# Attention chunks transposed by the DMA crossbar in place of TensorE, in a fused decay-attention and GELU-MLP kernel

## The chip, the cores and the metric

The kernel runs on one core of one Trainium2 chip. The metric is device time in microseconds for one launch; lower is better. Engines are written PE (TensorE), DVE (VectorE), ACT (ScalarE), POOL (GpSimd) and SP (SyncE, which here only issues DMAs).

## The reference

Linear attention with a per-head decay `lam`, in blocks, with a running state, then an MLP with exact GELU. Shapes: q, k, v are (4, 8, 768, 64); the MLP has 3072 tokens, 512 to 2048 to 512.

```python
for b in range(nb):
    qb, kb, vb = (q[:, :, sl], k[:, :, sl], v[:, :, sl])
    intra = np.einsum('bhic,bhjc->bhij', qb, kb) * Dmask[None]
    intra = np.einsum('bhij,bhjd->bhid', intra, vb)
    inter = np.einsum('bhid,bhde->bhie', qb * lam_pow[None], kv_state)
    out[:, :, sl] = intra + inter
    kb_dec = kb * rev_pow[None]
    kv_state = lam_block * kv_state + np.einsum('bhsd,bhse->bhde', kb_dec, vb)
x = out.transpose(0, 2, 1, 3).reshape(B * S, H * D)
h = x @ w_in
g = 0.5 * h * (1.0 + erf(h / sqrt(2)))
return g @ w_out
```

`Dmask[i, j]` is `lam ** (i - j)` for i >= j and 0 above; `lam_pow` is `lam ** (i + 1)`.

## The kernel before, in words

The sequence is cut into chunks of 128 positions of all 8 heads: 24 chunks, six per batch entry, so a chunk's place in its sequence `sb` runs from 0 to 5. Four chunks make a group (512 tokens), and there are six groups. The MLP works on one group at a time. While the MLP of group g runs, the attention of the four chunks of group g+1 is woven into it, so that TensorE always has matmuls to do. The four chunks of group 0 are done ahead (`early`).

A chunk has four steps:
- `begin`, kind 0: `prefetch(n + 4)` first issues the loads of q, k and v of the chunk four ahead on POOL's DMA queue (line 66; the load casts f32 to bf16). Then `decay_k` (L178) makes `k_dec` on POOL.
- `transposes`, kind 1: 8 TensorE transposes (L184), 4 of k and 4 of q (a pair of heads each), into a PSUM tile `t_ps`. DVE then copies the k half to `kT` (L190), and multiplies the q half by the row of decays `lam_q` into `qT` (L191).
- `scores`, kind 2: 8 matmuls `sc_ps` from `kT` and `qT` (L198), up to 8 matmuls `kv_ps` from `k_dec` and `v` (L205), the product with the mask on DVE (`sc_m`, L210), and the new state (L214 or L216). POOL then makes `old`, the decayed state, for the chunk after (L219); chunks with `sb` 4 and 5 have no `old`, and those with `sb` 5 no `k_dec`.
- `outputs`, kind 3: 8 matmuls from state and `qT` (L228), 8 from `v` and `sc_m` (L232), and a DVE cast into the MLP's input `x_t` (L238).

The MLP of a group is a list of 32 blocks of 4 matmuls: 16 blocks `mm1` (L250, each followed by a GELU on ACT, L252), then 16 blocks `mm2` (L262). Each four `mm2` blocks end one tile of 128 output rows, which ACT copies to SBUF (L267) and SP stores (L268, 256 KB).

The order of the instructions is the program's own, since the kernel runs under a manual schedule: each engine takes its instructions in the order in which they are written. A list `todo` gives each step of each chunk a position in the group's blocks. Chunk i's step with the fraction f stands at (i + f) of four equal intervals, which cover 97% of the group, so an interval is 7.76 blocks. Before each block, every step whose position has been reached is written out. For chunk i = 0 a negative fraction means the start of the group's list:

```python
at = lambda f: (first + (end - first) * (i + f) / M) * total
...
for run, cost in blocks:
    while todo and todo[0][0] <= done:
        _, kind, step = todo.pop(0)
        step(kind)
    run()
    done += cost
```

In groups g >= 1 of the loop, scores of chunk i stands at fraction 0.35: for the four chunks after 3, 11, 19 and 26 blocks. Outputs stand at 0.75. `kT`, `qT` and `k_dec` have three buffers each, the loaded q, k and v eight, and each engine waits only on semaphores, so POOL and SP may run ahead of TensorE.

Of the kernel before, what the change touches and what calls it, by code (L numbers as in the profile page):

```python
# [9 lines left out]
BF16 = mybir.dt.bfloat16  # L10
# [5 lines left out]
def kernel(  # L16
# [10 lines left out]
    nc = tc.nc  # L27

    B, H, S, D = q.shape
    d_model, d_ff = moe_w_in.shape  # L30
    C = 128
    NB = S // C
    NCH = B * NB
    HP = H // 2
# [15 lines left out]
    work_pool = ctx.enter_context(tc.tile_pool(name="work", bufs=3))  # L50
# [66 lines left out]
    lam_p = consts.tile([128, H], F32)  # L117
# [8 lines left out]
    for hi in range(2):  # L126
        p = slice(hi * D, (hi + 1) * D)
        nc.vector.tensor_copy(cpw[p], pw_r[p, :, :, hi])
    for b in range(LB):
        n = 2 ** b  # L130
# [24 lines left out]
    def bank(shape, dtype, tag, name):  # L155
        return ps.tile(shape, dtype, tag=tag, name=name, bufs=2 if tag in ("sc", "mh", "mo") else 1)

    def begin(n, early=False):
        c = Chunk()
        c.n, c.sb, c.early = n, n % NB, early  # L160
        c.sc_tag = "mo" if early and n % 2 else "sc"
        if n == 0:
            for name in "kq":
                raw[0, name] = qkv_pool.tile([128, H, D], BF16, tag=name, name=f"{name}_t")
                nc.scalar.copy(raw[0, name], first_f[name])  # L165
        c.q, c.k, c.v = (raw.pop((n, name)) for name in "qkv")
        return c

    def decay_k(c, eng):

        if c.sb == NB - 1:
            return
        c.k_dec = work_pool.tile([128, H, D], BF16, tag="kd", name="k_dec")
        if eng is nc.scalar:
            for h in range(H):
                nc.scalar.activation(c.k_dec[:, h, :], c.k[:, h, :], ACT.Copy, scale=lam_k[:, h:h + 1])
        else:
            eng.tensor_mul(c.k_dec, c.k, lam_k[:, :, None].to_broadcast((128, H, D)))  # L178

    def transposes(c):  # L180
        t_ps = bank([128, 2, HP, C], BF16, "mh" if c.early else "t", "t_ps")
        for i, src in ((0, c.k), (1, c.q)):
            for hp in range(HP):
                nc.tensor.transpose(t_ps[:, i, hp, :], src[:, 2 * hp:2 * hp + 2, :], ident)  # L184
        c.kT = work_pool.tile([128, HP, C], BF16, tag="kT", name="kT")
        c.qT = work_pool.tile([128, HP, C], BF16, tag="qT", name="qT")
        if c.early:
            nc.scalar.copy(c.kT, t_ps[:, 0])
        else:
            nc.vector.tensor_copy(c.kT, t_ps[:, 0])  # L190
        nc.vector.tensor_mul(c.qT, t_ps[:, 1], lam_q)  # L191

    def scores(c):
        sc_ps = [bank([128, HP, C], F32, c.sc_tag, f"sc_ps{hi}") for hi in range(2)]
        for hp in range(HP):
            for hi in range(2):
                p = slice(hi * D, (hi + 1) * D)
                nc.tensor.matmul(sc_ps[hi][:, hp, :], c.kT[p, hp, :], c.qT[p, hp, :], start=True, stop=True)  # L198
        more = c.sb < NB - 1
        if more:  # L200
            kv_ps = bank([128, HP, D], F32, "t", "kv_ps")
            for hp in range(HP):
                for hi in range(2):
                    h = 2 * hp + hi
                    nc.tensor.matmul(kv_ps[hi * D:(hi + 1) * D, hp, :], c.k_dec[:, h, :], c.v[:, h, :],  # L205
                                     start=True, stop=True)
        c.sc_m = work_pool.tile([128, HP, 2, C], BF16, tag="sc_m", name="sc_m")
        dmask_r = dmask.rearrange("p (hp hi) i -> p hp hi i", hi=2)
        for hi in range(2):
            nc.vector.tensor_mul(c.sc_m[:, :, hi, :], sc_ps[hi], dmask_r[:, :, hi, :])  # L210
        if more:
            new = work_pool.tile([128, HP, D], BF16, tag="state", name="state")
            if c.sb == 0:
                nc.vector.tensor_copy(new, kv_ps)  # L214
            else:
                nc.vector.tensor_add(new, kv_ps, states[c.n][1])  # L216
            old = work_pool.tile([128, HP, D], F32, tag="old", name="old")
            if c.sb < NB - 2:
                (nc.vector if c.early else nc.gpsimd).tensor_mul(old, new, lam_c_b)  # L219
            states[c.n + 1] = new, old  # L220

    def outputs(c, x_t, off):
        o_ps = bank([128, HP, C], F32, "o", "o_ps")
        if c.sb > 0:
            for hp in range(HP):
                for hi in range(2):
                    p = slice(hi * D, (hi + 1) * D)
                    nc.tensor.matmul(o_ps[p, hp, :], states[c.n][0][p, hp, :], c.qT[p, hp, :],  # L228
                                     start=(hp == 0), stop=False, skip_group_check=True)
        for hp in range(HP):  # L230
            for hi in range(2):
                nc.tensor.matmul(o_ps[hi * D:(hi + 1) * D, hp, :], c.v[:, 2 * hp + hi, :], c.sc_m[:, hp, hi, :],  # L232
                                 start=(c.sb == 0 and hp == 0), stop=True, skip_group_check=True)
        x_o = x_t[:, :, off * C:(off + 1) * C]
        if c.early:
            nc.scalar.copy(x_o, o_ps)  # L236
        else:
            nc.vector.tensor_copy(x_o, o_ps)  # L238
# [60 lines left out]
    def alloc_x(g):  # L299
        xT[g] = x_pool.tile([128, NK1, M * C], BF16, tag="x", name="x_t")  # L300
# [3 lines left out]
    def prefetch(upto):  # L304
        while next_load[0] <= min(upto, NCH - 1):
            for name in "kqv":
                load(next_load[0], name)
            next_load[0] += 1
# [3 lines left out]
    live = {}  # L312
    for s in range(M + 1):
        if s < M:
            live[s] = begin(s, early=True)
            if s == 2:
                load_w_in(0)
            transposes(live[s])
            decay_k(live[s], nc.scalar if s < 2 else nc.gpsimd)
            if s == 0:  # L320
                make_dmask()
        if s >= 1:
            outputs(live[s - 1], xT[0], s - 1)
        if s < M:
            scores(live[s])
# [5 lines left out]
    for g in range(NG):  # L331
        blocks = mlp_blocks(g)
        total = sum(c for _, c in blocks)
        todo = []
        if g + 1 < NG:
            alloc_x(g + 1)
            first, end = (0.77, 1.0) if g == 0 else (0.0, 0.97)
            for i in range(M):
                n = (g + 1) * M + i
                at = lambda f: (first + (end - first) * (i + f) / M) * total  # L340

                def step(kind, n=n, i=i):
                    if kind == 0:
                        prefetch(n + 4)
                        live[n] = begin(n)
                        decay_k(live[n], nc.gpsimd)
                    elif kind == 1:
                        transposes(live[n])
                    elif kind == 2:
                        scores(live[n])  # L350
                    else:
                        outputs(live[n], xT[g + 1], i)
                fs = (-0.3, 0.0, 0.4, 1.0) if g == 0 else (-0.3, 0.0, 0.35, 0.75)
                todo += [(at(f), kind, step) for kind, f in enumerate(fs)]
            todo.sort(key=lambda t: t[0])
        done = 0
# [6 lines that stand above are left out]
        for _, kind, step in todo:  # L363
            step(kind)
# [30 lines left out]
```

## Time and profile before

| | us |
|---|---|
| median of three runs | 242.4 (241.0 to 243.05) |
| profiled execution, whole | 242.4 |
| profiled execution, span of its instructions | 240.6 |
| PE busy in the span | 217.7 |
| POOL busy | 95.1 |
| DVE busy | 85.8 |
| ACT busy | 82.7 |

The span runs from the first to the last instruction of one profiled execution. Busy time is the time in which the engine has an instruction at work. In lines of groups or of the timeline, `kT<-t_ps` means that the tile left of the arrow is written from the one right of it; L190 is line 190 of the kernel; a bracket such as `[3.66 <-PE o_ps L262]` says how long the engine was idle before and what ended that. `SPq` is SP's queue of DMA issues. The MLP of group 1 starts at about 69 us, those of the later groups at 105, 140, 175 and 210 us; the tail of the program is the last group's MLP with no attention left in it.

### The profile page before, as it was taken

The numbers are of one execution on the slowest core, as the hardware profiler recorded it, in microseconds if no ns is written. First come the engines' busy times: TensorE is split into PE (matmuls) and PEld (weight loads), VectorE is DVE, ScalarE is ACT, GpSimd is POOL, SyncE is SP. The second block draws the span as 40 slices with busy tenths as digits, with TensorE's granted clock in tenths as the row PEclk, the third lists the DMA queues.
The fourth block names the chain that finished last, engine by engine and source line by source line (L and its number), as shares of the span: only waits on it lengthen the run. The fifth ranks groups of instructions, "written<-read, shape, count | busy, mean of one in ns | idle before, by whom it ended". The sixth has DMA issues, their size and how long they took to land.

```text
span 240.6 us, 4008 instructions
## 1 busy us (share of the span) xinstructions
PE 217.7 (90%) x1652; PEld 110.5 (46%) x1680; DVE 85.8 (36%) x180; ACT 82.7 (34%) x149; POOL 95.1 (40%) x114
## 2 busy tenths in 40 slices
PE   0378899998499999999999999999999999999994
PEld 0256344454254444455455455444454545444453
DVE  6987200057633423324344343343342344100000
ACT  3463266010025530135521035521055510166211
POOL 8986337970775296007347592007211200000000
PEclk9999999999869999999999999999999999999999
DMA  7999999995994799225598599009110002110022
GB/s 112 152 158 203 191 200 155 155 198 35 98 117 28 46 73 161 56 87 33 33 68 93 105 154 87 3 1 137 62 44 0 3 9 81 44 44 0 10 80 87
DMA packets 82865, 20.44 MB, mean 85 GB/s; under 512 B 75552, under 2 KB 79904, under 8 KB 82848
## 3 DMA queue, kind: packets, MB, share of 16 engines
q0 software_dynamic: 77024, 13.37, 74.4%
q1 hardware_dynamic: 4784, 6.56, 7.8%
q10 hardware_dynamic: 1040, 0.26, 0.5%
q8 instruction: 13, 0.21, 0.4%
q14 instruction: 4, 0.03, 0.0%
HBM read 27.27 MB, written 6.29 MB: 139 GB/s over the span
## 4 chain that ended last, share of the span: by engine, by line
PE 71%; POOL 12%; DMA 10%; issue 6%; ACT 0%; POOLq 0%
PE h_ps L250 29%; PE o_ps L262 28%; DMA w_out_t<-in_moe_w_out_dram 7%; POOL v_t L66 3%; PE t_ps L184 3%; DMA k_t<-in_k_dram 3%; POOL q_t L66 3%; PE o_ps L232 3%; PE o_ps L228 2%; PE sc_ps L198 2%; POOL k_t L66 2%; POOL k_dec L178 2%; PE kv_ps L205 2%; PE o_ps L277 1%; POOL w_in_t L93 1%
## 5 line engine op out<-in xcount | busy, mean ns | idle before, releaser
L250 PE MATMUL h_ps<-x_t,w_in_t 128*128 128x512 bf16 x371 | 88.8, 386 | 1.7 <-ACT x_t L236 0.7
L262 PE MATMUL o_ps<-w_out_t,g_t 128*128 128x512 bf16 x353 | 83.9, 383 | 1.4 <-issue 0.9
L252 ACT ACTIVATE g_t<-h_ps 128x512 bf16<-128x512 f32 x96 | 57.3, 597 | 45.1 <-PE h_ps L250 44.4
L250 PEld LDWEIGHTS <-w_in_t 128*128 128x128 bf16 x384 | 36.5, 99 | 43.3 <-issue 4.1
L262 PEld LDWEIGHTS <-g_t 128*128 128x128 bf16 x368 | 34.0, 98 | 37.9 <-issue 0.6
L267 ACT COPY o_sb<-o_ps 128x512 f32<-128x512 f32 x23 | 13.5, 585 | 92.8 <-PE o_ps L262 92.8
L210 DVE TENSOR_TENSOR sc_m<-sc_ps,dmask 128x512 bf16<-128x512 f32 x48 | 30.9, 686 | 31.4 <-PE sc_ps L198 31.3
L219 POOL TENSOR_TENSOR old<-state,cpw 128x256 f32<-128x256 bf16 x12 | 7.4, 613 | 81.4 <-DVE state L216 40.8
L238 DVE CAST x_t<-o_ps 128x512 bf16<-128x512 f32 x20 | 13.8, 692 | 38.7 <-PE o_ps L232 38.5
L190 DVE COPY kT<-t_ps 128x512 bf16<-128x512 bf16 x20 | 8.5, 423 | 48.6 <-PE t_ps L184 48.6
L66 POOL DMA_DIRECT2D v_t<-in_v_dram x24 | 21.5, 897 | 3.3 <-DMA w_out_t<-in_moe_w_out_dram 1.7
L66 POOL DMA_DIRECT2D q_t<-in_q_dram x23 | 20.5, 892 | 4.9 <-DMA w_out_t<-in_moe_w_out_dram 3.7
L66 POOL DMA_DIRECT2D k_t<-in_k_dram x23 | 20.9, 909 | 3.9 <-DMA w_out_t<-in_moe_w_out_dram 1.7
L178 POOL TENSOR_TENSOR k_dec<-k_t,lam_k 128x512 bf16<-128x512 bf16 x18 | 20.1, 1118 | 0.9 <-DMA k_t<-in_k_dram 0.7
L198 PE MATMUL sc_ps<-qT,kT 64*128 64x128 bf16 x192 | 10.4, 232 | 7.6 <-DVE qT L191 7.6
L191 DVE TENSOR_TENSOR qT<-t_ps,lam_q 128x512 bf16<-128x512 bf16 x24 | 16.3, 681 | 0.0
L184 PE MATMUL t_ps<-ident,k_t 128*128 128x128 bf16 x96 | 10.4, 238 | 5.9 <-DVE pw L124 5.9
L198 PEld LDWEIGHTS <-kT 64*128 64x128 bf16 x192 | 6.5, 99 | 16.1 <-issue 12.5
L184 PEld LDWEIGHTS <-k_t 128*128 128x128 bf16 x96 | 7.3, 104 | 10.3 <-ACT k_t L165 5.9
L232 PE MATMUL o_ps<-sc_m,v_t 128*64 128x128 bf16 x192 | 11.6, 243 | 0.2 <-DVE sc_m L210 0.2
L184 PE MATMUL t_ps<-ident,q_t 128*128 128x128 bf16 x96 | 10.5, 239 | 0.7 <-ACT q_t L165 0.7
L205 PE MATMUL kv_ps<-v_t,k_dec 128*64 128x64 bf16 x160 | 7.7, 213 | 2.2 <-POOL k_dec L178 2.2
(45 smaller groups left out, 80.3 us busy)
## 6 DMA issues: line engine op xcount, KB each, us to landing
out_dram<-o_sb SPq DMA_DIRECT2D x23, 256.0 KB, 2.0
v_t<-in_v_dram POOLq DMA_DIRECT2D x24, 128.0 KB, 4.9
k_t<-in_k_dram POOLq DMA_DIRECT2D x23, 128.0 KB, 4.7
q_t<-in_q_dram POOLq DMA_DIRECT2D x23, 128.0 KB, 5.0
w_in_t<-in_moe_w_in_dram POOLq DMA_DIRECT2D x4, 512.0 KB, 7.7
w_out_t<-in_moe_w_out_dram POOLq DMA_DIRECT2D x4, 512.0 KB, 15.1
k_first<-in_k_dram ACTq DMA_DIRECT2D x1, 256.0 KB, 4.5
q_first<-in_q_dram SPq DMA_DIRECT2D x1, 256.0 KB, 5.3
```

The source lines that it names most:

```text
L66: nc.gpsimd.dma_start(raw[n, name], chunk_of(name, n))
L178: eng.tensor_mul(c.k_dec, c.k, lam_k[:, :, None].to_broadcast((128, H, D)))
L184: nc.tensor.transpose(t_ps[:, i, hp, :], src[:, 2 * hp:2 * hp + 2, :], ident)
L191: nc.vector.tensor_mul(c.qT, t_ps[:, 1], lam_q)
L198: nc.tensor.matmul(sc_ps[hi][:, hp, :], c.kT[p, hp, :], c.qT[p, hp, :], start=True, stop=True)
L210: nc.vector.tensor_mul(c.sc_m[:, :, hi, :], sc_ps[hi], dmask_r[:, :, hi, :])
L232: nc.tensor.matmul(o_ps[hi * D:(hi + 1) * D, hp, :], c.v[:, 2 * hp + hi, :], c.sc_m[:, hp, hi, :], start=(c.sb == 0 and hp == 0), stop=Tru ...
L238: nc.vector.tensor_copy(x_o, o_ps)
L250: nc.tensor.matmul(h_ps, w_in_t[:, ki, kf * 128:(kf + 1) * 128], x_t[:, ki, :], start=(ki == 0), stop=(ki == NK1 - 1))
L252: nc.scalar.activation(g_t[:, kf, :], h_ps, ACT.Gelu)
L262: nc.tensor.matmul(om[io], g_t[:, kf, io * C:(io + 1) * C], w_out_t[:, kf, :], start=(kf == 0), stop=(kf == NK2 - 1))
L267: nc.scalar.copy(o_sb, om[io])
```

## The change

In the loop's passes g >= 1, which prepare groups 2 to 5 (chunks 8 to 23), the TensorE transposes and the two DVE operations after them are replaced by two DMA transposes on SP's queue. The decay of q, which was applied after the transposing, is applied before it, by POOL, with the column of decays `lam_p` in place of the row `lam_q`. The step that starts a chunk stands at the fraction -0.8 in these groups, not -0.3; the other positions stay. Groups 0 and 1 (chunks 0 to 7) are as before.

```diff
+    def dma_transposes(c):
+        c.kT = work_pool.tile([128, HP, C], BF16, tag="kT", name="kT")
+        c.qT = work_pool.tile([128, HP, C], BF16, tag="qT", name="qT")
+        q_hat = work_pool.tile([128, H, D], BF16, tag="qh", name="q_hat")
+        nc.sync.dma_start_transpose(out=c.kT, in_=c.k.rearrange("p h d -> p (h d)"))
+        nc.gpsimd.tensor_mul(q_hat, c.q, lam_p[:, :, None].to_broadcast((128, H, D)))
+        nc.sync.dma_start_transpose(out=c.qT, in_=q_hat.rearrange("p h d -> p (h d)"))
...
-                def step(kind, n=n, i=i):
+                def step(kind, n=n, i=i, g=g):
                     if kind == 0:
                         prefetch(n + 4)
                         live[n] = begin(n)
+                        if g > 0:
+                            dma_transposes(live[n])
                         decay_k(live[n], nc.gpsimd)
                     elif kind == 1:
-                        transposes(live[n])
+                        if g == 0:
+                            transposes(live[n])
...
-                fs = (-0.3, 0.0, 0.4, 1.0) if g == 0 else (-0.3, 0.0, 0.35, 0.75)
+                fs = (-0.3, 0.0, 0.4, 1.0) if g == 0 else (-0.8, 0.0, 0.35, 0.75)
```

The DMA transposes read SBUF and write SBUF: `kT` and `qT` have the same layout as before, 128 partitions (a pair of heads by 64) by 4 pairs by 128 positions.

## The prediction

> **What bounds the kernel now.** I read the page's busy times first, then the busy times by stage, then the chain of waits, and last the timeline around the four places where the chain could break. The first row of the page:
>
> ```profile
> PE 217.7 (90%) x1652; PEld 110.5 (46%) x1680; DVE 85.8 (36%) x180; ACT 82.7 (34%) x149; POOL 95.1 (40%) x114
> ```
>
> TensorE (PE) is busy for 90%, no other engine for half. The busy times by stage (cut at the first matmul of each MLP group) show how little is idle where the change acts:
>
> ```profile
> 105.30:140.20 34.90, 34.37 (x277) 17.06 (x280) 13.34 (x24) 11.84 (x21) 17.80 (x21) 1.00 0.73 72
> 140.20:174.90 34.70, 34.33 (x271) 16.89 (x274) 13.00 (x23) 11.87 (x21) 11.61 (x14) 1.00 0.70 70
> 174.90:209.60 34.70, 34.33 (x271) 16.79 (x274) 13.00 (x23) 11.67 (x20) 3.23 (x4) 1.00 0.09 31
> ```
>
> The columns are span, PE, weight load, DVE, ACT, POOL, clock, DMA share and GB/s. PE works 34.3 of 34.7 us at clock 1.00, so whatever is taken from its stream shortens the stage, and whatever it waits for lengthens it. The chain of waits confirms it; this is the boundary at 139.9 us:
>
> ```profile
> 138.20 1.67 PE o_ps L262 x7
> 139.88 0.45 PE t_ps L184 x8
> 140.32 2.59 PE h_ps L250 x12
> 142.91 0.33 PE sc_ps L198 x8
> 143.24 0.25 PE kv_ps L205 x8
> ```
>
> Each piece starts when the one before ends. Eight transposes of a chunk cost 0.445 us (0.056 each; the 238 ns of one in the table of groups is latency, not cost). After the boundary, three MLP blocks (12 matmuls, 2.59 us) are all that lies before the first chunk's scores.
>
> [...] a 256 KB store landed after 2.0 us beside nothing and after 3.4 us beside loads.
>
> **The change, part by part.**
>
> Removed from PE: 8 transposes for each of 16 chunks (8 to 23). Fifteen times 0.445 us is on the chain. At the first one (chunk 8, 68.8 us) the next matmul at 69.6 waited anyway for the x_t cast, which ends at 69.53, so it gives some 0.1. Sum: 15 x 0.445 + 0.1 = 6.8 us.
>
> Removed from DVE: 16 copies of 423 ns and 16 products of 681 ns, 17.7 us. DVE is busy 13 of 35 us per stage; this gives nothing to the chain.
>
> Added to POOL: 16 products q_hat of the same shape as k_dec, 1118 ns each, 17.9 us. POOL is busy at most 18 us of a stage. In its queue q_hat stands behind the chunk's three load issues (0.9 us each) and ahead of k_dec and of the next `old`. For chunks 1 to 3 of a group this is covered. The tightest is chunk 1 in the stage at 140 us: POOL ends the first chunk's step at about 140.7 (the 139.6 at which k_dec ends before, and 1.1), then three issues and q_hat make 144.5; with 3.4 us for the pair of transposes (below) qT is there at 148, and its scores come at 151.7: 3.7 us of cover. For the group's first chunk it matters once, below.
>
> Added to SP: 32 crossbar transposes of 128x512, two a chunk. They come in program order 0.8 of a chunk's interval ahead, 1.15 intervals (9.7 us) before the scores that read them. But a group's list cannot reach back before its own start. For the first chunk of a group the -0.8 is clipped to block 0, and scores comes after block 2 as before. SP's stores are in the same queue. For chunks 1 to 3 SP runs ahead of PE, with no store of this group before them, and I count their transposes at nothing; if one pair took over about 7 us that cover would be gone. For the first chunk the queue's last entry is the store of the group before, which waits for the last mm2 matmul and its copy on ScalarE:
>
> ```profile
> 105.00 0.58 ACT L267 COPY o_sb<-o_ps 128x512 f32<-128x512 f32 x1 [3.66 <-PE o_ps L262]
> 105.20 2.75 PE L250 MATMUL h_ps<-x_t,w_in_t 128*128 128x512 bf16 x11
> 105.40 0.42 DVE L190 COPY kT<-t_ps 128x512 bf16<-128x512 bf16 x1 [1.58 <-PE t_ps L184]
> 105.61 0.33 SPq L268 DMA_DIRECT2D out_dram<-o_sb  x1
> ...
> 107.89 0.40 PE L198 MATMUL sc_ps<-qT,kT 64*128 64x128 bf16 x8
> ```
>
> SP is free at 105.61 + 0.33 = 105.94. Without the transposes the scores are due at 107.95 - 0.45 = 107.50. Only 1.56 us remain for two crossbar transposes. That is the new wait; queued behind it on PE is everything, since PE runs in order.
>
> What two transposes take: the DMA share of that store, sampled from 105 to 108 in slices of 75 ns, shows the flight of a DMA from SP:
>
> ```profile
> DMA  0000000000000000000699999989400000000000
> ...
> out_dram<-o_sb SPq DMA_DIRECT2D x1, 256.0 KB, 2.0
> ```
>
> Data move from 106.43 to 107.15 us; so 0.33 issue, 0.5 until the first byte, 0.7 for 256 KB, 0.45 until it counts as landed. For a transpose of 128 KB I take 0.5 + 0.45 + 0.45 = 1.4 us after its issue (0.35 of data at the store's rate, a little more for the crossbar). [...] I take 1.0 us, an estimate[...]. Two issues and one flight: 1.0 + 1.0 + 1.4 = 3.4 us.
>
> Stalls of PE at the four first chunks:
> - 104.9 us (chunk 12): 105.94 + 3.4 - 107.50 = 1.8 us.
> - 174.6 us (chunk 20): SP free at 175.62, due at 177.63 - 0.45 = 177.18, no loads in flight: 1.8 us.
> - 139.9 us (chunk 16): SP free at 140.90, due at 142.46, and the DMA engines are full of loads; the store there landed 1.4 us later, which I add: 140.90 + 3.4 + 1.4 - 142.46 = 3.2 us.
> - 68.8 us (chunk 8): here POOL decides. Its queue before:
>
> ```profile
> 67.03 0.92 POOL L66 DMA_DIRECT2D k_t<-in_k_dram  x1
> ...
> 67.94 0.89 POOL L66 DMA_DIRECT2D q_t<-in_q_dram  x1
> ...
> 68.82 0.88 POOL L66 DMA_DIRECT2D v_t<-in_v_dram  x1
> ...
> 69.71 1.06 POOL L178 TENSOR_TENSOR k_dec<-k_t,lam_k 128x512 bf16<-128x512 bf16 x1
> ```
>
> q_hat takes the place of k_dec and ends at 70.8; issue and flight 2.4, and 1.0 for the loads (that store landed in 3.0 against 2.0 us): 74.2. The scores are due at 72.89 - 0.1 = 72.8. Stall 1.4 us. k_dec then ends at 71.9, in time.
>
> Sum of stalls 1.8 + 1.8 + 3.2 + 1.4 = 8.2 us, rounded to 8.3 with the wake-ups. Net: 8.3 - 6.8 = +1.5 us. The profiled execution took 242.4 us around a span of 240.6; the median of the runs shown is also 242.4. Forecast: 243.9 us, span 242.1. Twelve chunks gain, four give it back.
>
> **Rivals.**
>
> A, the forecast: gain 6.8, four stalls of about 2 us, 241 to 246 us.
>
> B, short stalls: [...]stalls 0.7, 0.7, 1.5 and 0.4 with half of the contention, sum 3.3, net -3.5: 238.9 us. For it: SP's plain issue is 0.33 us, and in the stage at 174.6 the DMA engines are idle.[...]
>
> C, slower than before: a pair of transposes takes longer than 4 us from SP's free moment to landing, and PE waits for it at each of the four boundaries. One mechanism, with its place at sc_ps L198 of chunks 8, 12, 16 and 20. It decides from a mean stall above (6.8 + 2.4)/4 = 2.3 us, that is about 0.25 us above my mean. [...]the stalls are 3.1, 3.1, 4.5 and 2.3: 13.0, net +6.2: 248.6 us. For it: loads fill the DMA engines at two of the four boundaries[...]. Against it: the store's data are out by 107.15, before a transpose's could start.
>
> D, [...] Stalls of 9 us at four places[...], so chunks 1 to 3 fall late too: 37 us and more of stalls, some 272 us. If the rearranged copy should not go through the crossbar at all, it would be later still; I count that here.
>
> **How the numbers follow.** Chances: A 0.50, B 0.16, C 0.26, D 0.08. A measurement of this kernel tells about 1% (2.4 us; the runs shown lie from 241.0 to 243.05). B is faster; A divides into 0.34 within 1% and 0.16 slower; C and D are slower. Faster 0.16, same 0.34, slower 0.50. A's own range is 241 to 246; the whole one, from B's value to a little above C's, is 239.0 to 250.0, with D and the far end of C left out.
>
> **What would show it.** Right: PE's busy time falls by about 7 us (128 matmuls fewer, of 0.056 each); the chain shows sc_ps waiting for a DMA in four places only; the first chunk's scores in each of four groups come 1.4 to 3.2 us late; SP's two issues take about 1 us each. Wrong: a wait for the crossbar at chunks 1 to 3; no wait at the boundaries (B); a landing time of 4 us and more with idle DMA engines (C); or waits for POOL's k_dec or `old` on the chain.

## The result, and the profile after

The changed kernel takes 254.6 us (median of four runs, 252.2 to 255.2) against 241.7 us for the kernel before: a ratio of 1.0508, 95% interval 1.0421 to 1.0594. That is slower, and above the range of the forecast. (The 241.7 is the median of four runs, three of which are those of the table ahead.) Two executions of the runs below were over 1.5% slower than the fastest of their kernel and are left out of its ratio; one of them is the profiled execution of the kernel without the last loads, from which only waits and what directly follows them are read. The span of the profiled execution grew from 240.6 to 252.6 us, by 12.0 us. The first row of its page:

```profile
PE 216.8 (86%) x1528; PEld 104.9 (42%) x1552; DVE 69.5 (28%) x148; ACT 82.7 (33%) x149; POOL 111.1 (44%) x130
```

PE has 124 recorded matmuls less and is busy for only 0.9 us less, where the forecast had about 7. Two things follow: PE is idle for 14% of a longer span, not 10%, and its remaining matmuls must have become slower. From the list of waits (total, times, longest):

```profile
PE sc_ps L206 <- DMA qT<-q_hat: 12.0, 4, 6.3
```

and from the list of DMA issues (count, and the median us to landing):

```profile
kT<-k_t SPq DMA_TRANSPOSE x16, 2.9
qT<-q_hat SPq DMA_TRANSPOSE x16, 3.2
```

Four waits, at the first chunk of each of the four groups, as forecast; together 12.0 us. At the boundary of chunk 12 the timeline shows how the pair of transposes queues:

```profile
106.59 0.33 SPq L276 DMA_DIRECT2D out_dram<-o_sb  x1
...
107.03 1.22 SPq L197 DMA_TRANSPOSE kT<-k_t  x1
...
108.35 1.21 SPq L199 DMA_TRANSPOSE qT<-q_hat  x1
...
110.93 0.40 PE L206 MATMUL sc_ps<-qT,kT 64*128 64x128 bf16 x8 [2.44 <-DMA qT<-q_hat]
```

The store is issued first, then each transpose holds SP for 1.2 us (1.32 from one start to the next), and the second one landed 2.4 us after its issue began. The chain of waits at the next boundary, chunk 16, shows the longest wait and what comes after it:

```profile
143.21 1.74 PE h_ps L258 x8
144.95 0.60 SPq L197
...
145.66 6.29 DMA qT<-q_hat
...
152.08 0.61 PE sc_ps L206 x8
152.69 0.36 PE kv_ps L213 x8
153.05 4.04 PE h_ps L258 x12
```

Here the second transpose alone takes 6.29 us from the start of its issue to its landing. And the 12 matmuls behind the scores take 4.04 us, where 12 such matmuls took 2.59 to 2.69 us in the kernel before. The busy times by stage around the wait of chunk 12 (span, then PE, PEld, DVE, ACT, POOL, and after them the clock) say why:

```profile
108.00:111.00 3.00, 0.56 (x7) 0.10 (x6) 0.00 (x0) 0.86 (x2) 0.00 (x0) 1.00 0.54 112
111.00:115.00 4.00, 4.00 (x25) 1.66 (x25) 1.62 (x3) 0.60 (x1) 1.96 (x3) 0.57 0.48 93
115.00:118.00 3.00, 2.95 (x21) 1.34 (x20) 0.69 (x1) 1.79 (x3) 2.99 (x4) 1.00 1.48 95
```

PE is busy for 0.56 of the 3 us of the first stretch, and in the four microseconds after it the granted clock is 0.57: it fell to a half and came back. The slow matmuls are those, and this price was not in the forecast.

### The profile page after: what moved, and what is told of

Read it like the earlier page. It is cut to its first block, busy times and chain, and to the rows that moved or that the text cites. A ratio compares the mean times of both kernels' runs of the same rounds, so it can differ in the third digit from the quotient of the medians.

```text
span 252.6 us, 3812 instructions
## 1 busy us (share of the span) xinstructions
PE 216.8 (86%) x1528; PEld 104.9 (42%) x1552; DVE 69.5 (28%) x148; ACT 82.7 (33%) x149; POOL 111.1 (44%) x130
## 3 DMA queue, kind: packets, MB, share of 16 engines
HBM read 27.27 MB, written 6.29 MB: 133 GB/s over the span
## 4 chain that ended last, share of the span: by engine, by line
PE 74%; DVE 7%; issue 6%; DMA 6%; POOL 3%; SPq 1%; ACT 0%; POOLq 0%; DVEq 0%
PE h_ps L258 34%; PE o_ps L270 30%; DMA qT<-q_hat 6%; PE sc_ps L206 3%; PE o_ps L240 3%; PE o_ps L236 2%; PE kv_ps L213 1%; DVE sc_m L218 1%; PE o_ps L285 1%; POOL v_t L66 1%; DVE qT L191 1%; POOL k_dec L178 1%; DVE old L227 1%; SPq L197 1%; POOL q_t L66 1%
## 5 line engine op out<-in xcount | busy, mean ns | idle before, releaser
L258 PE MATMUL h_ps<-x_t,w_in_t 128*128 128x512 bf16 x372 | 94.2, 406 | 2.4 <-DVE x_t L246 0.8
L270 PE MATMUL o_ps<-w_out_t,g_t 128*128 128x512 bf16 x356 | 82.9, 383 | 1.5 <-issue 1.4
L258 PEld LDWEIGHTS <-w_in_t 128*128 128x128 bf16 x384 | 38.3, 103 | 50.4 <-issue 13.2
L198 POOL TENSOR_TENSOR q_hat<-q_t,lam_p 128x512 bf16<-128x512 bf16 x16 | 16.9, 1057 | 0.1
L236 PE MATMUL o_ps<-qT,state 64*64 64x128 bf16 x160 | 9.1, 240 | 0.0
L184 PE MATMUL t_ps<-ident,k_t 128*128 128x128 bf16 x32 | 4.0, 264 | 6.0 <-DVE pw L124 6.0
L236 PEld LDWEIGHTS <-state 64*64 64x64 bf16 x160 | 5.6, 116 | 8.1 <-issue 8.0
L240 PEld LDWEIGHTS <-v_t 128*64 128x64 bf16 x192 | 7.0, 119 | 4.1 <-issue 2.5
```

Source lines behind the costliest of these rows:

```text
L198: nc.gpsimd.tensor_mul(q_hat, c.q, lam_p[:, :, None].to_broadcast((128, H, D)))
L258: nc.tensor.matmul(h_ps, w_in_t[:, ki, kf * 128:(kf + 1) * 128], x_t[:, ki, :], start=(ki == 0), stop=(ki == NK1 - 1))
L270: nc.tensor.matmul(om[io], g_t[:, kf, io * C:(io + 1) * C], w_out_t[:, kf, :], start=(kf == 0), stop=(kf == NK2 - 1))
```

## Experiments

Theory 1, made after the result: the loss is the four waits at the boundaries (from the clipped position behind the last store, and from flights beside loads), and a stretch of half clock after each; the other 12 chunks do gain. Rivals: the crossbar's traffic slows the rest of the kernel; the chunk-16 wait has another cause; or the slow matmuls have nothing to do with the wait.

**The first chunks back on TensorE.**

```diff
-                        if g > 0:
+                        if g > 0 and i > 0:
                             dma_transposes(live[n])
...
-                        if g == 0:
+                        if g == 0 or i == 0:
                             transposes(live[n])
```

> The changed kernel, but the first chunk of each of groups 2 to 5 (8, 12, 16, 20) is transposed by TensorE as before; 12 chunks keep the crossbar. Theory 1 (the four boundary waits and a clock that falls to half after each of them are the whole loss; the other 12 chunks gain 0.445 us each): no wait for qT<-q_hat on the chain, no low clock after 75 us, 12 x 0.445 = 5.3 us below before, about 236.5 us. Rival (the crossbar's traffic or SP's and POOL's longer queues slow the rest as well): less than 2 us below before, or above it, with waits or slower matmuls at chunks 1 to 3 of a group.

Measured: 236.2 us, ratio 0.977 (0.972 to 0.981). No wait of PE for the crossbar, and no low clock after 72 us. By the ratio that is 5.6 us for 12 chunks, 0.47 each: the forecast's gain per chunk (0.445) is right, and twelve crossbar chunks beside everything else cost nothing that can be told, although their transposes landed after 3.3 to 3.4 us in the median and 7.9 at the longest. The rival of a general slowdown falls.

**The first chunk's starting step issued earlier.** The whole step moves: loads, transposes and `k_dec` of chunks 12, 16 and 20.

```diff
-                todo += [(at(f), kind, step) for kind, f in enumerate(fs)]
+                todo += [(at(f), kind, step) for kind, f in enumerate(fs)
+                         if not (kind == 0 and i == 0 and n >= 12)]
+                if i == M - 1 and g + 2 < NG and n + 1 >= 12:
+                    todo.append((at(0.2), 0, lambda kind, step=step, n=n, g=g:
+                                 step(kind, n=n + 1, i=0, g=g + 1)))
```

> The changed kernel, but the starting step of chunks 12, 16 and 20 is written out in the group before, before its block 25, ahead of that group's last two stores in SP's queue; chunk 8 stays as in the changed kernel. Theory 1 (the wait comes from the clipped position, behind the last store): the waits of 2.4, 6.3 and 2.4 us and three stretches of half clock (1.6 us each) go, 11.1 + 4.9 = 16 us less than the changed kernel, about 238.5 us; what is left over the best case is chunk 8's. Rival (the crossbar is too slow or too contended near a boundary, wherever it is issued): a wait of 2 us or more stays at chunk 16 and the total stays above 243.

Measured: 236.8 us, ratio 0.980 (0.974 to 0.985), 1.7 us better than expected. SP's queue and the chain at the boundary of chunk 12 now read:

```profile
97.62 1.22 SPq L197 DMA_TRANSPOSE kT<-k_t  x1
98.96 1.19 SPq L199 DMA_TRANSPOSE qT<-q_hat  x1
101.06 4.58 SPq L276 DMA_DIRECT2D out_dram<-o_sb  x2
```

```profile
104.62 2.59 PE h_ps L258 x12
107.21 0.33 PE sc_ps L206 x8
107.54 0.24 PE kv_ps L213 x8
107.78 2.69 PE h_ps L258 x12
```

The pair leaves 8 us before the scores, ahead of the last two stores, and nothing waits. So the position of the starting step in the list made three of the four waits, not the crossbar as such. Chunk 8's wait of 0.8 us is still there.

**Useless matmuls in the place of the wait.**

```diff
                     elif kind == 2:
+                        if i == 0 and n > 2 * M:
+                            f_ps = bank([128, M * C], F32, "mh", "f_ps")
+                            for _ in range(28 if n == 16 else 11):
+                                nc.tensor.matmul(f_ps, w_in_t[:, 0, 0:128], xT[g][:, 0, :],
+                                                 start=True, stop=True)
                         scores(live[n])
```

> The changed kernel with useless TensorE matmuls of 128x512 ahead of the scores of chunks 12, 16 and 20 (11, 28 and 11 of them, 2.4, 6.1 and 2.4 us, which is what PE waits there now); their results are not used. Theory 1 (part of the loss is the clock that falls to half after the wait): PE has 50 matmuls more to do and the kernel is still faster, by three times 1.6 us, about 249.7 us; the clock stays at 1.00 after 105 us. Rival (the slow matmuls after the wait come from the crossbar's traffic in SBUF, or from the wait itself): no faster than the changed kernel, about 254.6 us or more.

Measured: 249.1 us, ratio 1.0308 (1.0253 to 1.0362), against 1.0508 for the changed kernel: 0.020 of 242 us, 4.8 us less, by fifty matmuls more. The chain at chunk 12:

```profile
105.42 2.59 PE h_ps L258 x12
108.01 2.39 PE f_ps L364 x11
110.40 0.05 issue
110.44 0.40 PE sc_ps L206 x8
110.84 0.24 PE kv_ps L213 x8
111.09 2.69 PE h_ps L258 x12
```

The crossbar runs as before and the scores come as long after the boundary as in the changed kernel, but the 12 matmuls after them take 2.69 us, not 4.28, and the clock is at 1.00 from 104 to 116 us. The slow matmuls come from PE standing still, not from the transposes' traffic.

**The same waits without a crossbar.** In the kernel before, two, three or six useless DVE products stand between `kT` and `qT` of chunks 12, 16 and 20:

```diff
+        if c.n in (12, 16, 20):
+            for _ in range(2):   # 2, 3 or 6
+                junk = work_pool.tile([128, H, C], F32, tag="junk", name="junk", bufs=1)
+                nc.vector.tensor_mul(junk, dmask, dmask)
         nc.vector.tensor_mul(c.qT, t_ps[:, 1], lam_q)
```

> The kernel before (TensorE transposes, no crossbar), with two useless DVE products of 128x1024 f32 (1.2 us each) between kT and qT of chunks 12, 16 and 20. qT is ready 1.45 us ahead of its scores in the kernel before, so PE waits 2.4 - 1.45 = 1.0 us at three places. Theory 1 with a threshold (a wait of 0.8 us left the clock alone at chunk 8 of the changed kernel): three waits and no low clock after 100 us, 2.9 us above before. Rival (any wait costs a stretch of half clock): 2.9 + 4.9 = 7.8 us above.

> As d2_delay with three such products: PE waits 3.6 - 1.45 = 2.2 us at three places, with no crossbar transpose in the kernel. Theory 1 (the half clock comes from PE's wait, whatever it waits for): 6.5 us of waits and three stretches of half clock at 1.6 us, 11.4 us above before. Rival (the slow matmuls come from the crossbar's traffic): 6.5 us above before, clock at 1.00.

> As d2_delay with six such products: PE waits 7.3 - 1.45 = 5.8 us at three places. Theory 1 with a price that doesn't grow with the wait: 17.4 + 4.9 = 22.3 us above before, the clock back at 1.00 some 3.3 us after each wait. Rival (the clock's price grows with the wait): over 25 us above before.

Measured: 245.1, 252.3 and 268.1 us against 243.1; ratios 1.0106 (1.0044 to 1.0168), 1.0397 (1.0338 to 1.0456) and 1.1048 (1.0976 to 1.112), so 2.6, 9.7 and 25.5 us more. With two products PE waits 0.92, 1.64 and 0.92 us, and the 12 matmuls after the scores take 2.70, 2.69 and 2.70 us, so the clock stays up, as theory 1 with a threshold had it. With three it waits 2.18, 2.90 and 2.18 us, and in the profiled execution the clock fell at the first two places; the profile at the first and the last:

```profile
108.00:110.00 2.00, 0.00 (x0) 0.00 (x0) 1.97 (x3) 0.60 (x1) 0.00 (x0) 1.00 0.00 0
110.00:112.00 2.00, 1.85 (x22) 1.00 (x23) 1.51 (x4) 0.20 (x1) 0.00 (x0) 0.92 0.03 8
112.00:115.00 3.00, 3.00 (x8) 0.81 (x6) 0.20 (x1) 0.99 (x2) 2.73 (x4) 0.50 0.20 13
...
185.00:188.00 3.00, 0.82 (x6) 0.30 (x5) 2.90 (x3) 1.17 (x2) 0.00 (x0) 1.00 0.01 1
188.00:191.00 3.00, 3.00 (x28) 1.50 (x27) 1.62 (x3) 1.10 (x2) 0.90 (x2) 1.00 0.00 0
```

At 112 us PE has been back at work for almost two microseconds when the clock is at a half, and the last wait, as long, costs no clock at all. The traces show a pattern that fits. Between 60 and 200 us of the changed kernel the clock switches at 63.6, 73.8, 111.4, 114.8, 148.9, 155.8, 189.9 and 193.3 us: 3, 11, 1, 10, 2, 10 and 1 intervals of 3.41 us apart. In the kernel with three products it falls at 111.68 and is back at 115.09. Cut at this grid, the first and the last wait of the kernel with three products differ:

```profile
108.27:111.68 3.41, 1.53 (x21) 0.92 (x22) 2.92 (x4) 0.33 (x1) 0.00 (x0) 1.00 0.02 5
111.68:115.09 3.41, 3.41 (x11) 0.94 (x11) 0.52 (x2) 1.19 (x2) 2.81 (x4) 0.50 0.23 15
...
183.36:186.77 3.41, 2.44 (x12) 0.98 (x11) 3.34 (x4) 1.86 (x4) 0.00 (x0) 1.00 0.21 77
186.77:190.19 3.42, 2.21 (x24) 1.22 (x24) 2.78 (x5) 0.56 (x1) 0.09 (x1) 1.00 0.00 0
```

The first wait leaves PE idle for 1.88 us of one interval, and the next one runs at half clock. The last wait is split into 0.97 and 1.21 us, and the clock stays up. At chunks 12, 16 and 20 of all traces the clock, where it was up, fell after intervals with 1.88 us or more of idle PE. It stayed through waits of 1.64 us or less, and where the grid left at most 1.45 us of a wait in one interval. So the length of a wait of this size does not decide alone; its place in the grid seems to, though no run moved a wait in the grid and nothing else. How many intervals are lost differs between executions: an interval at half clock lowers the mean clock of an execution of 250 us by 0.007 (half of 3.41 us in 250), and mean clocks of 0.973, 0.980 and 0.980 in three executions of this kernel are worth 4, 3 and 3 of them.

With six products the 12 matmuls after the three waits took 4.48, 4.40 and 5.19 us against 2.70, and the waits came to 19.3 us rather than 17.4 (5.96, 7.40 and 5.96), at chunk 16 because two of the products took 1.96 us, not 1.24. The price of the clock is then 2.1 to 2.9 us a place with the slower scores: a little more than after the shorter waits, but not in proportion to the wait. The total, 25.5 us, lies where the rival had it (over 25), but 1.9 us of that are longer waits; neither expectation met it exactly.

**Loads moved away from the boundary.**

```diff
-                        prefetch(n + 4)
+                        if g == 0:
+                            prefetch(n + 4)
...
                         outputs(live[n], xT[g + 1], i)
+                        if g > 0 and i < 2:
+                            prefetch((g + 2) * M + 2 * i + 1)
```

> The changed kernel, with the loads of the chunks four ahead issued after the outputs of the first and second chunk of a group, so that few loads are in flight at a group's boundary. Theory 1 (the crossbar pair lands in 2.4 us on idle DMA engines and in up to 6.7 beside loads, which makes the wait at chunk 16): the wait at chunk 16 falls from 6.3 to about 2.4 us and that at chunk 8 from 0.8 to about 0; 4 to 5 us less than the changed kernel, about 250 us; the half clock after each wait stays. Rival (chunk 16's wait has another cause, for instance POOL's late q_hat): that wait stays near 6 us and the total near 254.6.

Measured: 254.0 us, ratio 1.0486 (1.0422 to 1.055), no gain that can be told. The edit missed its aim at chunk 16: nothing in POOL's queue waits for PE at these steps, so POOL ran ahead and issued all twelve loads of the last four chunks from about 140 to 153 us, in the middle of the boundary. The flight of `qT` grew to 8.0 us and the wait with it to 8.1. At chunk 8, where the loads did move away, the wait of 0.8 us went. Both point to the loads, but neither is a clean test. At chunk 20 PE waited 2.44 us again, and this time the clock stayed up: the grid cut the wait into 0.99 and 1.45 us.

**The last loads left out.**

```diff
+    kept = {}
...
+        if n >= 20:
+            raw[n, name] = kept[n - 4, name]
+            return
         raw[n, name] = qkv_pool.tile([128, H, D], BF16, tag=name, name=f"{name}_t")
+        kept[n, name] = raw[n, name]
         nc.gpsimd.dma_start(raw[n, name], chunk_of(name, n))
```

> The changed kernel without the loads of q, k and v of chunks 20 to 23, whose work is done on the tiles of chunks 16 to 19; so no load is in flight when chunk 16 is transposed. Theory 1 (its wait of 6.3 us is the crossbar's landing time beside loads): the pair lands in 2.4 us each, the wait at chunk 16 falls to 2.4 us, 3.9 us less than the changed kernel, about 250.7 us. Rival (the wait has another cause at that boundary): the wait stays above 5 us and the total near 254.6.

Measured: 249.9 us, ratio 1.0273 (1.0195 to 1.035), near the 250.7 expected. From its chain at chunk 16:

```profile
145.71 0.60 SPq L202
...
146.42 2.42 DMA qT<-q_hat
...
148.97 0.40 PE sc_ps L211 x8
149.37 0.24 PE kv_ps L218 x8
149.62 4.38 PE h_ps L263 x12
```

Without loads in flight the transpose lands in 2.4 us, not 6.3, and the half clock after the wait stays (4.38 us for 12 matmuls). The longest wait was the flight beside loads.

**Chunk 8, and a version that beats both.** First the early version with chunk 8 back on TensorE:

```diff
-                        if g > 0:
+                        if g > 0 and n > 2 * M:
                             dma_transposes(live[n])
...
-                        if g == 0:
+                        if g == 0 or n == 2 * M:
                             transposes(live[n])
```

Then, on top, chunk 7's `k_dec` ahead of the three load issues of its step:

```diff
-                        prefetch(n + 4)
+                        if n != 2 * M - 1:
+                            prefetch(n + 4)
                         live[n] = begin(n)
...
                         decay_k(live[n], nc.gpsimd)
+                        if n == 2 * M - 1:
+                            prefetch(n + 4)
```

> e2_early with chunk 8 transposed by TensorE again, so the crossbar serves 15 chunks, 9 to 23. Theory 1 with its part on chunk 8 (its eight transposes filled the time in which the MLP waits for x_t and let the clock come back at 70.7 us; without them it came back at 73.4, and the scores waited 0.8 us): 0.8 us of wait and about 1.4 us of half clock go, for next to nothing of added work: 2.2 us less than e2_early, about 234.6 us. Rival (chunk 8's transposes cost what others cost): the wait of 0.8 us goes and 0.45 us of work comes, about 0.4 us less than e2_early.

> e5_early_c8_pe, and k_dec of chunk 7 is made ahead of the three load issues of its step on POOL's queue, not behind them; a wait of 2.2 us of PE for k_dec at about 65 us, which was in the kernel before too, and the half clock after it should go. Theory 1 (a wait costs itself and a stretch of half clock): 2.2 + 2 us less than e5_early_c8_pe, about 230.5 us. Rival (a wait costs itself alone): 2.2 us less, about 232.4 us.

Measured: 236.5 us, ratio 0.975 (0.970 to 0.980), and 233.1 us, ratio 0.964 (0.960 to 0.968). For chunk 8 the medians say little (0.4 us, and 1.2 us by the ratios); the first would fit the rival. One trace of each kernel says more, from the start of `kv_ps` of chunk 7 to the start of chunk 8's scores:

| kernel | kv_ps of chunk 7 | sc_ps of chunk 8 | between |
|---|---|---|---|
| before | 65.43 | 72.83 | 7.4 |
| changed | 65.29 | 75.15 | 9.9 |
| loads moved away (no wait there) | 64.40 | 73.41 | 9.0 |
| early | 64.11 | 73.86 | 9.8 |
| early, chunk 8 on TensorE | 65.05 | 72.70 | 7.7 |
| and k_dec first | 62.94 | 68.38 | 5.4 |

Without its eight transposes chunk 8 loses 2.1 to 2.5 us, which is theory 1's 2.2 and not the rival's 0.4. But theory 1 added up two things that overlap. The chain of the changed kernel at this place runs through the crossbar, not through the slow matmuls:

```profile
70.67 4.35 DMA qT<-q_hat
75.02 0.14 issue
75.15 0.40 PE sc_ps L206 x8
```

Had the clock come back as early as before, the scores would by this chain have waited for the landing all the same. And with the loads moved away, where nothing waits, the half clock alone puts them 9.0 us after `kv_ps`, 1.6 more than before. Each of the two is enough for most of the loss, and putting the transposes back removes both. Each row of the table is one execution: by the mean clocks, the early version had 2 to 3 intervals at half clock in its four executions, the version with chunk 8 on TensorE 1 to 2 in its six. That may be why the totals differ by less than the traces; the latter's program had also reached this place 0.9 us later than the early one's.

The last version removes a wait that the kernel before had too (2.2 us of PE for `k_dec` at 65 us). It gained 3.4 us by the medians, between the gains of 4.2 and 2.2 that were expected (both totals were expected too low, from a start of 234.6). A new wait of 0.7 us for chunk 8's `k_dec` came in its place. Its clock is 1.00 throughout its span: it is the fastest kernel of this study, 8.7 us below before in the medians of that comparison.

## Why the prediction was wrong

The mechanism that the forecast named held, and so did its place: four waits, clipped to the group's start, behind the last store. The sum failed in three terms; the last column, all but its first row read from the trace, adds up to about the growth of the span:

| term | forecast us | measured us |
|---|---|---|
| 15 chunks without transposes | -6.7 | -6.7 (15 x 0.445, near the first experiment's rate) |
| chunk 8: scores later, net of its transposes | +1.3 | +2.5 (0.8 of it a wait) |
| chunks 12 and 20: wait | +1.8 each | +2.44 each |
| chunk 16: wait | +3.2 | +6.28 |
| half clock after the waits of 12, 16, 20 | none | +5.2 |
| wake-ups | +0.1 | in the waits |
| sum | +1.5 | +12.2 (span: +12.0) |

The half clock of 5.2 us is worked out from the chain: the 12 matmuls after the scores took 4.28, 4.04 and 4.38 us against 2.70, and scores with `kv_ps` 0.1, 0.4 and 0.1 us more.

**The step that failed most** is the one that priced a wait at its own length. The forecast read the clock column (1.00 in all three stages) and took it as given, though it belonged to a PE that was idle for only 0.4 to 0.5 us of each stage. It was there to be seen: the only dip that the clock row of the kernel before shows is at 60 to 72 us, and in it lies PE's wait of 2.2 us for `k_dec`:

```profile
PEclk9999999999869999999999999999999999999999
...
PE kv_ps L205 <- POOL k_dec L178: 2.2, 1, 2.2
```

The price of the pause was 5.2 of the 10.7 us between forecast and measurement, and the filler and delay experiments tie it to the wait, whatever the wait is for. What makes the clock fall is not shown beyond that. A gap of 2.4 us cost a half-clock stretch at both boundaries where it occurred in the changed kernel (and none at chunk 20 with the loads moved), one of 2.2 us at one of two places.

**The second** is the contention term, taken from stores beside loads (1.4 us more than beside nothing at chunk 16, 1.0 at chunk 8). In the changed kernel the store at chunk 16 landed after 2.7 us, while the two transposes issued behind it needed 5.4 and 6.3; at chunk 8 `qT` needed 4.4, not 3.4. A store was a poor stand-in: some 2.5 us too little at chunk 16, about 1 at chunk 8. On idle DMA engines a 128 KB transpose landed in 2.4 us against 2.0 for a 256 KB store, which is near; beside loads the 5.4 and 6.3 us stand against 2.7. Why a transpose suffers more than a store is not shown.

**The third** is the issue time, 1.0 us taken, an estimate that rested on no trace, and 1.32 measured from start to start; together with 0.1 between the store and the first transpose, and 0.1 from landing to PE, it turns the 1.8 into 2.44, and adds some 0.6 us at chunk 16 as well. The flight on idle engines was forecast at 2.4 us from the issue (1.0 + 1.4) and measured at 2.4.

At chunk 8 the small size of the wait, 0.8 us against 1.4, is luck: `qT` landed about 1 us later than forecast, and PE, slowed by the half clock, came later too. The forecast saw that the MLP's first matmul there waits for the x_t cast anyway, and booked the transposes as nearly free to keep or drop. In fact they were work that kept PE busy while the clock came back: before, it was at 1.00 from 70.7 us, after two intervals at half; without them, with a gap of 0.78 us in their place, from 73.8 us, after three. "Gives nothing" was not the whole of it: with no wait left, their going still made the scores 1.6 us later.

Of the rivals, whose issue times rested on no trace either, C came nearest. The mean wait was 3.0 us, above the 2.3 from which C decides. But a pair needed 3.9 us from SP's free moment to landing at chunks 12 and 20, just under C's 4 us; at chunk 16 it was longer (7.7 us), by the loads, and at chunk 8 POOL's `q_hat` came between. And the waits alone (12.0 us) would have given 242.4 + 12.0 - 6.8 = 247.6 us; the rest was the clock, which C did not have either. B and D fell.

## What to carry to other kernels

When PE bounds a kernel and runs in order, price a new wait of two microseconds or more at its length plus, quite possibly, a stretch of half clock after it. Here an interval of work at half clock lost 1.7 us, half of its 3.41 (12 matmuls and the scores at chunk 12: 1.58 and 0.1 us). Waits of 2.2 and 2.4 us brought it in some places and not in others, those of 5.96 to 8.1 us at all five places, those of 0.92 and 1.64 us at none. And look in the profile before for a dip after a wait that is there already. A step moved "ahead" by a fraction of an interval is ahead only as far as its list reaches back; look where the first item of each list lands and what stands before it in its queue. Moving transposes off PE paid in full (0.47 us a chunk measured, 0.445 forecast) where they left early enough, and the first item of a group could as well stay on PE.

## What the runs showed of the hardware

- From 60 to 200 us of the changed kernel the clock switched only at whole numbers of 3.41 us from one another, and its stretches at half lasted 3.4, 6.8 or 10.2 us. At chunks 12, 16 and 20 it fell at the end of an interval in which PE had been idle for 1.88 us or more, even if PE was back at work by then (idle from 108.0, back at 110.15, half clock from 111.7 us in the kernel with three products), and held through waits of 1.64 us or less. Equal waits of 2.18 us cost it once and spared it once.
- A 128x512 bf16 crossbar transpose inside SBUF held SP's queue for 1.2 us in most cases (1.19 to 1.61 in the changed kernel) and landed 2.4 us after the start of its issue with idle DMA engines. At the boundaries of chunks 8 and 16, beside loads that cast on POOL's queue, it took 4.4 (`qT` of chunk 8 in the changed kernel) to 8.0 (`qT` of chunk 16 with the loads moved).
- A DVE product of 128x1024 f32 took 1.23 or 1.24 us, but one or two of those at chunk 16 took 1.95 or 1.96 in each of the three kernels with added products. Why is not shown.
